# Where attention ends and the MLP begins: the last unit's maxima, four output pieces and one pair of PSUM banks

## The chip, the cores and the metric

The kernel runs on one core of one Trainium2 chip. The metric is the device time of one execution in microseconds (us); the time of a kernel is the median of its timed runs. Beside them one more execution is recorded by the hardware profiler. Its rows have a start, a duration, an engine, a source line of the kernel and the tiles written and read. The engines are PE (TensorE), DVE (VectorE), ACT (ScalarE), POOL (GpSimd) and SP, whose queue starts most DMAs. Each engine works through its own queue in order.

## The reference

One transformer block with adaptive layer norm: attention over the last 512 keys of a cache, then a gated MLP, both added to the residual. Inputs and outputs are float32; D = 576, 2048 queries, 32 query heads on 16 key heads of 128, F = 4608.

```python
mod = (silu(c) @ w_mod).reshape(1, 6, 1, D)           # sa, ca, ga, sb, cb, gb
h = layernorm(x) * (1 + ca) + sa
q = (h @ wq), 32 heads; k, v = last 512 rows of the caches, each head twice
p = softmax(q k^T * 128 ** -0.5)
x = x + ga * ((p v) @ wo)
h = layernorm(x) * (1 + cb) + sb
gate = h @ W_gate; up = h @ W_up
x = x + gb * ((max(gate, 0) * up) @ W_down)
```

## The kernel before

**Precision.** A float32 operand is cut into a rounded part (hi, type fp32r, made by ACT) and the remainder (lo, made by POOL as raw minus hi). A product takes three matmuls: hi by hi, hi by lo, lo by hi.

**Attention.** 128 units, one for each head and each block of 512 queries, u = 0 to 127 (NU = 128). Unit u makes its scores transposed, keys on partitions: two PSUM tiles `s{u}_0` and `s{u}_1` of two banks each, 12 matmuls (lines 462 to 464). DVE reduces them to the maximum of each query (467, 475, 476), PE spreads it over the partitions (490), and `max_bc` (503 to 522) makes of it a tile with the maximum of each query in every partition. `exp_half` (528 to 542) then takes the maxima off and exponentiates, by one of two ways, which `by_pe(u)` chooses:

- PE: the maxima are cut into two parts (512 to 514), transposed (515), rounded by ACT (518), and four matmuls with a matrix of minus ones subtract them inside the PSUM banks (533). ACT's exponential reads the banks (535).
- DVE: one transpose (520), then one DVE subtraction for each half, from PSUM to SBUF (537). ACT's exponential works in SBUF (539).

In this kernel PE does it for u = 0, 1 and for u = 127 (`PE0, PE1 = 2, 1`), DVE for the other 125. After that ACT rounds p to hi (526), DVE and POOL sum over the keys (552, 555), POOL makes lo (546), PE multiplies with V into a `pv` bank (564 to 566) one unit later, DVE divides by the sum (`o_mul`, 572), ACT and POOL cut the result (576 `ohi`, 580 `olo`).

**Output pieces.** `wo_piece(u, q)` multiplies the results of units u - 1 and u (two heads) for 128 queries with two gated blocks of `wo`: 12 matmuls into the pair of banks `psW` (591), then the sum goes to the residual tile `acc`: DVE adds (602), or the bank was filled with `acc` by ACT first (624, a seed) and ACT copies it back (600).

**MLP.** Products of 512 rows and one block of weights, for gate and for up: in each stage m (0 to 35) seven of them, in the order P1, P6, P2, P7, P5, P4, P3, in a Strassen-like scheme in which P2 goes on accumulating in P1's banks and P3 in P5's. A product has two halves (`prod`, line 1046, 7 matmuls each, one for gate and one for up). DVE or ACT then takes it out (`evac`; 1067 or 1069 to 1071 for the gated products P2, P5, P4, P3, of which 1071 is the last; 1175 and 1178 for P6 and P7). ACT and POOL cut the gated result (1061, 1062). Weights of stage m = 1 and after are summed by DVE (852), then cut by ACT (822) and POOL (823, 824). Down products `md_piece` (591, 602) of stage m - 1 stand between the products of stage m.

**The seam.** In stage m = 0 a product's two halves share one tile of two banks, taken from a list:

```python
npair, px, free, kind = [0], {}, ["s", "s"], {}          # 1142
k = free.pop(0)                                          # 1155, in new_banks
free.append(kind[m, s])                                  # 1472, after evac of P6, P2, P7, P4, P3
```

`"s"` means a tile of the pool that held the scores (two tiles, four banks). Stage 0 has no down products, so output pieces that attention left over fill in (`filler`): first three of units 124 and 125, then four of units 126 and 127. The four can only come after the end of unit 127, so the steps are interleaved by hand: P1, P6, then `pv` of unit 127, P2, then `last_unit` (line 1483: spread of the sums, reciprocal 495, transpose 500, `o_mul` 572), `o_hi`, `o_lo`, then `open_x` (1489), which closes the pool of the two banks that held `pv127` and the last spread, `qm128`, opens the pool "x" on these two banks, appends "x" to the list and puts the four pieces into `filler`. P7, P5, P4 and P3 follow. From m = 1 on, `open_g` (1144) replaces the score pool by banks "a" and "b", and "x" and `psW` take the down products in turn.

So P7 took a score pair, P5 the other one and P4 took "x"; the piece of each product stood between its two halves; and P1 of stage 1 (`gh_P`) begins on the pair that P5 and P3 used.

Of the kernel before, what the change touches and what calls it, by code (L numbers as in the profile page):

```python
# [23 lines left out]
EPS = 1e-5  # L24
SCALE = float(P) ** -0.5
H2 = D // 2
PE0, PE1, MLP0 = 2, 1, 8
NLAST = 5


# [1 line left out]
def kernel(  # L32
# [573 lines left out]
    def wo_piece(u1, qt, seed=None):  # L606
        g, qb, h = unit(u1)
        return down_piece([ohi[u1 - 1], ohi[u1]], [olo[u1 - 1], olo[u1]], [wos[h - 1], wos[h]],
                          4 * qb + qt, qt, f"wo{u1}_{qt}", seed=seed)
# [39 lines left out]
    def md_piece(m, k, qt, pool=None):  # L649
        b, fp = divmod(m, NFP)  # L650
        i = 8 * b + 4 * k + qt
        down_piece([hhi[m, f, k] for f in range(2)], [hlo[m, f, k] for f in range(2)],
                   [ds_[m, f] for f in range(2)], i, qt, f"md{m}_{k}_{qt}", pool=pool)()
        if fp == NFP - 1:
            nc.sync.dma_start(out[i * P:(i + 1) * P, :], acc[i])
# [28 lines left out]
    def fast_pieces(m):  # L684
        return ([lambda n=n: fast_piece(m, "4", n) for n in range(2)] +
                [lambda k=k, n=n: fast_piece(m, k, n) for k in ("16", "75", "23") for n in range(4)])
# [83 lines left out]
    def order(m):  # L770
        return ("P1", "P6", "P2", "P7", "P5", "P4", "P3")
# [6 lines left out]
    def flush_stores(left=0, eng=None):  # L778
        while len(stores) > left:
            dst, src = stores.pop(0)  # L780
            (eng or nc.scalar).dma_start(dst.bitcast(F32), src.bitcast(F32))
# [255 lines left out]
    def prod(m, s, n, xx):  # L1037

        hs, w = hop[m // NFP, OPS[s][1]], wop[n]
        ps = pair[m, s][:, xx, :] if m < NG else pair[m, s][xx]  # L1040
        ops = []
        for t in range(2):
            ops += [(w[:, xx, t, :], hs[t]), (w[:, xx, 3 + t, :], hs[t]), (w[:, xx, t, :], hs[3 + t])]
        ops.append((w[0:96, xx, 2, :], hs[2][0:96]))
        for i, (a, c) in enumerate(ops):
            nc.tensor.matmul(ps, a, c, start=s not in ("P2", "P3") and i == 0, stop=i == len(ops) - 1,  # L1046
                             skip_group_check=True)
# [53 lines left out]
    def evac_half(m, s, x):  # L1101
        ps, fast = pair[m, s][x], m in FAST
        if s == "P1":
            if x == 0:
                tmp[m, "q"] = pp.tile([P, 2, 512], F32, tag="hi", name=f"q{m}")
            nc.scalar.copy(tmp[m, "q"][:, x, :], ps)
            if x and m - 1 in FAST:
                fast_last(m - 1)
            return
        q = tmp[m, "q"]  # L1110
        if s == "P6":
            nc.vector.tensor_tensor(q[:, x, :], ps, q[:, x, :], op=ALU.add)
            return
        if s == "P7":
            if x == 0:
                tmp[m, "r"] = pp.tile([P, 2, 512], F32, tag="lo", name=f"r{m}", bufs=2)
            nc.vector.tensor_tensor(tmp[m, "r"][:, x, :], ps, q[:, x, :], op=ALU.add)
            if x:
                nc.scalar.copy(q[:, 1, :], ps)
            return  # L1120
        if s == "P2" and x == 0:
            tmp[m, "r22"] = xp.tile([P, 640], F32, tag="xm", name=f"r{m}")[:, :512]
        if s == "P5" and x == 0:
            tmp[m, "c"] = pp.tile([P, 2, 512], F32, tag="lo", name=f"c22_{m}", bufs=2)
        f, k, r, a, op1 = {"P2": lambda: (0, 0, tmp[m, "r22"], None, ALU.add),
                           "P5": lambda: (1, 1, tmp[m, "c"][:, 0, :], tmp[m, "r"], ALU.add),
                           "P4": lambda: (1, 0, tmp[m, "r"][:, 0, :], tmp[m, "r"], ALU.add),
                           "P3": lambda: (0, 1, q[:, 0, :], q, ALU.subtract)}[s]()
        gated_half(x, ps, r, a, op1)
        if x == 0:  # L1130
            return
        if not fast:
            h_out(m, f, k, r)
        elif s == "P2":
            fast_split(m, "A22", r)
        elif s == "P5":
            fast_split(m, "A11", r)
        elif s == "P4":
            fast_later(m)


    npair, px, free, kind = [0], {}, ["s", "s"], {}
# [6 lines left out]
    def md_pool():  # L1149
        px["n"] = px.get("n", 0) + 1  # L1150
        return (px["x"], "x") if px["n"] % 2 else (psW, "w")
# [6 lines left out]
    def new_pair(m, s):  # L1158
        if m < NG:
            pair[m, s], kind[m, s] = new_banks(f"gu{npair[0]}")  # L1160
            return
        if "g" not in px:
            open_g()
        kind[m, s] = "ab"[(s in ("P6", "P7", "P4")) ^ m % 2]
        pair[m, s] = [px["g"].tile([P, 512], F32, tag=kind[m, s], name=f"gh{m}_{s}_{i}") for i in range(2)]
# [245 lines left out]
    for i in range(4):  # L1411
        m = 2 + 2 * i
# [10 lines left out]
    def sums(m, i):  # L1423

        for k, s in {1: [(0, "S1")], 2: [(0, "S4")], 5: [(1, "S3")], 6: [(1, "S2")]}.get(i, []):
            if 0 < m + k < NFP:
                w_sums(m + k, s)

    def others(m, i):
        w_prep(7 * m + i + 2)  # L1430
        for fn in mextra.pop((m, i - 1, False), []):
            fn()
        for ij in {2: [(1, 0)], 3: [(0, 0)], 4: [(1, 1)], 5: [(0, 1)]}.get(i, []):
            if m + 1 < NFP:
                w_load(m + 1, *ij)

    def mlp_slots():
        for m in range(NB):
            md = [lambda k=k, qt=qt: md_piece(m - 1, k, qt, md_pool())
                  for k in range(2) for qt in range(4)] if m else []  # L1440
            if m - 1 in FAST:
                md = fast_pieces(m - 1)
            for i, s in enumerate(order(m)):
                flush_stores()
                if s not in ("P2", "P3"):
                    new_pair(m, s)
                else:
                    pair[m, s], kind[m, s] = (x[m, {"P2": "P1", "P3": "P5"}[s]] for x in (pair, kind))
                prod(m, s, 7 * m + i, 0)
                if m or i:  # L1450
                    sums(m, i)
                    others(m, i)
                if m >= NG:
                    evac_half(m, s, 0)
                if m and i or m - 1 in FAST:
                    md.pop(0)()
                elif filler and not m:
                    filler.pop(0)()
                for fn in mextra.pop((m, i - 1, True), []):
                    fn()  # L1460
                prod(m, s, 7 * m + i, 1)
                wop.pop(7 * m + i)
                if m >= NG:
                    evac_half(m, s, 1)
                if m and i < 2 or m - 1 in FAST:
                    md.pop(0)()
                elif filler and not i:
                    filler.pop(0)()
                if m < NG:
                    evac(m, s)  # L1470
                if s not in ("P1", "P5") and m < NG:
                    free.append(kind[m, s])
                yield
        for k in range(2):
            for qt in range(4):
                md_piece(NB - 1, k, qt, md_pool())
        flush_stores()
        assert not mextra and not filler

    filler = [lambda q=q: wo_piece(NU - 3, q)() for q in (1, 2, 3)]  # L1480
    mlp = mlp_slots()

    def last_unit():
# [5 lines left out]
    def open_x():  # L1489
        psM_scope.__exit__(None, None, None)  # L1490
        px["x"] = ctx.enter_context(tc.tile_pool(name="psX", bufs=1, space=bass.MemoryType.PSUM,
                                                 reuse_waits="tile"))
        free.append("x")
        filler.extend([lambda q=q: wo_piece(NU - 1, q)() for q in range(4)])


# [49 lines left out]
    step("T.ohi", e + 5, o_hi, NU - 1)  # L1546
    step("T.olo", e + 5, o_lo, NU - 1)
    step("open", e + 6, open_x)

    sched.sort(key=lambda x: x[:2])  # L1550
# [131 lines left out]
```

## Time and profile before

| what | value |
|---|---|
| timed runs | 2923.57, 2925.33, 2927.05 us; median 2925.33 us |
| profiled execution | 2923.07 us, span 2921.3 us |
| mean granted TensorE clock | 0.994 |
| PE busy | 2852.1 us, 98% of the span |
| DVE / ACT / POOL busy | 76% / 49% / 75% |
| HBM | 149 GB/s over the span |
| seam | unit 127's scores begin at 1625.7 us, P1 of stage 1 at 1682.27 us |

The profile's span runs from the first to the last instruction; the execution's own time is 1.8 us longer. A row's bracket tells how long its engine stood idle before it and what released it. PE rows overlap: a matmul of 512 columns lasts 0.39 us, the next starts 0.23 us after it. "Granted clock" is the share of its full clock that TensorE was given in a stretch.

### The profile page before, as it was taken

The page shows a single profiled execution, that of the slowest core. Times are in us where ns is not written, and L with a number is a line of the kernel's source. Part 1 is how long each engine was busy: PE and PEld are TensorE (multiplying, and loading weights), DVE is VectorE, ACT ScalarE, POOL GpSimd, SP SyncE. Part 2 cuts the span into 40 slices and gives each one's busy share as a digit, 9 for nine tenths or more (in the row PEclk, how much of TensorE's full clock was granted, in tenths as well). Part 3 has the DMA queues.
Part 4 walks back from the last instruction along what each step waited for, and adds up shares of the span by engine and source line. Part 5 has one row for each costly group of instructions (what it writes and reads, how often), then busy time and mean ns, then how long its engine had stood idle before and what let it go on. Part 6 is the DMA issues. An engine that isn't in the chain of part 4 may idle for free.

```text
span 2921.3 us, 41631 instructions
## 1 busy us (share of the span) xinstructions
PE 2852.1 (98%) x15206; PEld 2481.5 (85%) x15206; DVE 2211.8 (76%) x3106; ACT 1431.5 (49%) x2023; POOL 2197.3 (75%) x1598
## 2 busy tenths in 40 slices
PE   6899999999999999999999999999999999999999
PEld 4678888888888888888888788888888888888888
DVE  7778888888878888777889677788887566666665
ACT  4666666666676666666656433333333122222221
POOL 5678888888888889876778666677888487777773
PEclk9999999999999999999999999999999999999999
DMA  5222222222223223322143355666767844444443
GB/s 211 87 95 73 83 93 84 67 100 92 92 85 107 88 66 125 109 70 86 66 132 128 118 191 201 218 221 239 263 246 260 319 152 160 153 153 154 154 145 137
DMA packets 165900, 410.62 MB, mean 141 GB/s; under 512 B 15040, under 2 KB 61888, under 8 KB 165696
## 3 DMA queue, kind: packets, MB, share of 16 engines
q1 hardware_dynamic: 132944, 289.23, 30.7%
q10 hardware_dynamic: 32752, 118.73, 10.3%
q8 instruction: 121, 1.98, 0.3%
q14 instruction: 83, 0.68, 0.1%
HBM read 275.81 MB, written 160.40 MB: 149 GB/s over the span
## 4 chain that ended last, share of the span: by engine, by line
PE 83%; POOL 5%; DVE 4%; ACT 3%; DMA 2%; issue 2%; SPq 0%; ACTq 0%; POOLq 0%; DVEq 0%
PE gh_P L1046 23%; PE wo L591 13%; PE qps L388 12%; PE md L591 7%; PE mf L672 6%; PE s L463 3%; PE s L464 3%; PE s L462 3%; PE pv L566 3%; PE pv L565 3%; PE pv L564 3%; POOL lo L546 1%; DMA hx_T<-hb 1%; PE qm L490 1%; DVE t L467 1%
## 5 line engine op out<-in xcount | busy, mean ns | idle before, releaser
L546 POOL TENSOR_TENSOR lo<-p,hi 128x1024 fp32r<-128x1024 f32 x256 | 611.0, 2408 | 2.6 <-ACT hi L526 2.6
L555 POOL TENSOR_TENSOR ks<-ks,p 128x512 f32<-128x512 f32 x256 | 344.1, 1344 | 281.4 <-ACT p L539 210.6
L467 DVE TRANSPOSE_TENSOR_REDUCE t<-s 128x32 f32<-128x1024 f32 x256 | 316.2, 1243 | 133.2 <-PE s L464 122.2
L1046 PE MATMUL gh_P<-hop_B,wop 128*128 128x512 f32 (+1 forms) x1470 | 368.8, 394 | 2.4 <-DVE q L1071 2.4
L1046 PE MATMUL gh_P<-hop_T,wop 128*128 128x512 f32 (+1 forms) x1246 | 315.9, 393 | 0.8 <-DMA wop<-wk_P 0.8
L1046 PEld LDWEIGHTS gh_P<-hop_B,wop 128*128 128x128 f32 (+1 forms) x1470 | 268.4, 189 | 52.7 <-issue 2.8
L537 DVE TENSOR_TENSOR p<-s,mb 128x1024 f32<-128x1024 f32 x250 | 295.3, 1218 | 4.2
L591 PE MATMUL wo<-woga,ohi 128*128 128x288 f32 x1344 | 282.2, 303 | 6.3 <-POOL woga L180 3.8
L388 PE MATMUL qps<-hTa,wA 128*128 128x512 f32 x1176 | 283.9, 393 | 2.3 <-DVE hTa L372 1.7
L526 ACT CAST hi<-p 128x1024 fp32r<-128x1024 f32 x256 | 269.1, 1051 | 7.0
L539 ACT ACTIVATE p<-p 128x1024 f32<-128x1024 f32 x250 | 264.1, 1056 | 16.3 <-DVE p L537 14.4
L388 PEld LDWEIGHTS qps<-hTa,wA 128*128 128x128 f32 x1176 | 222.5, 189 | 49.2 <-ACT lfa L370 2.7
L591 PE MATMUL md<-wogb,hhi 128*128 128x288 f32 x1280 | 260.3, 296 | 0.0
L1046 PEld LDWEIGHTS gh_P<-hop_T,wop 128*128 128x128 f32 (+1 forms) x1246 | 225.3, 188 | 41.1 <-DMA wop<-wk_P 1.2
L442 ACT ACTIVATE qhi<-qps 128x512 fp32r<-128x512 f32 x128 | 76.4, 597 | 340.4 <-PE qps L388 336.9
L591 PEld LDWEIGHTS wo<-woga,ohi 128*128 128x128 f32 x1344 | 219.8, 190 | 14.3 <-POOL woga L180 4.4
L591 PEld LDWEIGHTS md<-wogb,hhi 128*128 128x128 f32 x1280 | 214.0, 188 | 12.1
L591 PE MATMUL wo<-woga,olo 128*128 128x288 f32 x672 | 198.9, 296 | 0.4 <-POOL olo L580 0.2
L602 DVE TENSOR_TENSOR acc<-md,acc 128x576 f32<-128x576 f32 x160 | 120.4, 753 | 101.1 <-PE md L591 100.6
L591 PE MATMUL md<-wogb,hlo 128*128 128x288 f32 x640 | 188.9, 295 | 0.0
L600 ACT COPY acc<-wo 128x576 f32<-128x576 f32 x232 | 147.6, 636 | 68.6 <-PE wo L591 62.2
L580 POOL TENSOR_TENSOR olo<-rb,ohi 128x512 fp32r<-128x512 f32 x128 | 167.0, 1305 | 16.3 <-ACT ohi L576 11.3
(282 smaller groups left out, 7288.7 us busy)
## 6 DMA issues: line engine op xcount, KB each, us to landing
wop<-wk_P SPq DMA_DIRECT2D x133, 640.0 KB
wk_P<-wop ACTq DMA_DIRECT2D x119, 640.0 KB
wr<-wlay SPq DMA_DIRECT2D x68, 384.0 KB
againq<-akq SPq DMA_DIRECT2D x22, 640.0 KB
againo<-ako SPq DMA_DIRECT2D x18, 576.0 KB
rogb<-wd SPq DMA_DIRECT2D x36, 288.0 KB
rwA<-wq SPq DMA_DIRECT2D x32, 320.0 KB
wlay<-wg SPq DMA_DIRECT2D x36, 256.0 KB
```

The lines of the kernel that those rows point to most:

```text
L388: return [lambda i=i, a=a, b=b: nc.tensor.matmul(ps, a, b, start=(i == 0), stop=(i == n - 1)) for i, (a, b) in enumerate(ops)]
L467: nc.vector.tensor_reduce(t4[u][:, 2 * h:2 * h + 2, :].rearrange("p k b -> p (k b)"), t.rearrange("p k (b j) -> p (k b) j", j=32), axis=AX ...
L526: nc.scalar.copy(hi_[u, h], pt[u, h])
L537: nc.vector.tensor_tensor(p, t, bc[u][:, None, :].to_broadcast([P, 2, 512]), op=ALU.subtract)
L539: nc.scalar.activation(p, p, AF.Exp, bias=0.0, scale=1.0)
L546: nc.gpsimd.tensor_sub(lo_[u, h], pt[u, h], hi_[u, h].bitcast(F32))
L555: nc.gpsimd.tensor_tensor(ks_[u], ks_[u], p[:, j, :], op=ALU.add)
L580: nc.gpsimd.tensor_sub(olo[u], o.pop(u), ohi[u].bitcast(F32))
L591: nc.tensor.matmul(ps[:, half, :H2], a[:, sl], w[b][:, cs], start=(n == 0 and seed is None), stop=(n == 5), skip_group_check=seed is not None)
L600: nc.scalar.copy(av, ps[:, :, :H2])
L672: nc.tensor.matmul(ps[:, j, :H2], x[:, sl], w[:, c:c + H2], start=i == 0, stop=i == 2)
L1046: nc.tensor.matmul(ps, a, c, start=s not in ("P2", "P3") and i == 0, stop=i == len(ops) - 1, skip_group_check=True)
```

## The change

Three edits, all at the seam. No DMA, buffer size or matmul of the MLP changes.

1. `PE1` goes from 1 to 0: for u = 127 too, the DVE way of taking the maxima off.
2. The four late output pieces stand behind the second half of P7, P5, P4 and P3, ahead of the product's `evac`, where they stood behind the first half. The three early pieces stay where they were.
3. `open_x` puts "x" at the head of the list. P7 takes "x", P5 and P4 the score pairs; P3 uses P5's.

```diff
-PE0, PE1, MLP0 = 2, 1, 8
+PE0, PE1, MLP0 = 2, 0, 8
...
                 if m and i or m - 1 in FAST:
                     md.pop(0)()
-                elif filler and not m:
+                elif filler and not m and i < 3:
                     filler.pop(0)()
...
                 if m and i < 2 or m - 1 in FAST:
                     md.pop(0)()
-                elif filler and not i:
+                elif filler and not m and (i == 0 or i > 2):
                     filler.pop(0)()
...
-        free.append("x")
+        free.insert(0, "x")
```

## The prediction, made before the run

> **What bounds the kernel now.** I read the page first, then who waited for whom on PE around the seam and behind it, then the timeline row by row, then the granted clock microsecond by microsecond.
>
> ```profile
> PE 2852.1 (98%) x15206; PEld 2481.5 (85%) x15206; DVE 2211.8 (76%) x3106; ACT 1431.5 (49%) x2023; POOL 2197.3 (75%) x1598
> ...
> PE 83%; POOL 5%; DVE 4%; ACT 3%; DMA 2%; issue 2%; SPq 0%; ACTq 0%; POOLq 0%; DVEq 0%
> ```
>
> PE is busy 98% of the span and carries 83% of the chain that ended last. Only what shortens PE's work or its waits counts. PE's waits from 1600 to 1720 us (total, times, longest), the four largest that bear on the change:
>
> ```profile
> PE gh_P L1046 <- DVE q L1071: 2.4, 1, 2.4
> PE wo L591 <- ACT ohi L576: 1.6, 1, 1.6
> PE wo L591 <- ACT acc L600: 1.1, 1, 1.1
> PE wo L591 <- POOL olo L580: 0.8, 1, 0.8
> ```
>
> All those after 1690 us:
>
> ```profile
> PE gh_P L1046 <- POOL wop L824: 1.3, 3, 0.8
> PE mf L672 <- POOL fp_S L699: 0.9, 1, 0.9
> PE gh_P L1046 <- DMA wop<-wk_P: 0.8, 1, 0.8
> ```
>
> The seam holds several waits; the 1200 us behind it hold 3.0 us in all. So a shift of PE at the seam should reach the end almost whole, and the change can be worth a few microseconds, 0.1 to 0.3%. A change under about 0.2% (5.85 us) can't be told from none in a measurement of this kernel.
>
> **Part one: unit 127's maxima by DVE.** Unit 126 does it the DVE way:
>
> ```profile
> 1620.27 0.67 DVE L520 STREAM_TRANSPOSE mb<-r 128x512 f32<-128x512 f32 x1
> 1620.97 2.36 DVE L537 TENSOR_TENSOR p<-s,mb 128x1024 f32<-128x1024 f32 x2
> ```
>
> Unit 127 does it by PE:
>
> ```profile
> 1631.93 1.62 DVE L512 CAST rh<-r 128x16 fp32r<-128x16 f32 x1
> 1634.62 0.62 ACT L518 CAST mr<-mb 128x512 fp32r<-128x512 f32 x1 [6.32 <-DVE mb L515]
> 1634.37 0.40 PE L566 MATMUL pv<-lo,againv 128*128 128x512 f32 x1
> 1636.90 1.02 ACT L535 ACTIVATE p<-s 128x1024 f32<-128x1024 f32 x1
> 1640.91 0.63 ACT L600 COPY acc<-wo 128x576 f32<-128x576 f32 x1
> 1641.60 0.54 PE L591 MATMUL wo<-againo,ohi 128*128 128x288 f32 x2 [1.08 <-ACT acc L600]
> ```
>
> Removed: three small DVE operations (the cast alone 1.62 us), an ACT copy, four matmuls. Added: the two subtractions, 2.36 us. After the change the transpose starts where the cast did, 1631.93; 0.70 later (1620.27 to 1620.97) the first subtraction, which takes half of 2.36, 1.18; the exponential starts at 1633.85 instead of 1636.90. Two things could hold it. ACT: before it stand unit 125's cast, a copy back and a seed, three operations like the 0.63 of L600. They stood behind the ACT copy of the maxima, before which ACT idled 6.32 us; with that copy gone they wait only for the previous output piece, which PE ended before its twelve `pv` matmuls (12 x 0.23, a product's 3.22 / 14, before 1634.6: about 1631.8), so they end by 1633.7. DVE: what is queued behind the subtractions needs the exponential itself. So the gain there is 3.05 us. From the exponential to PE's next wait the chain on ACT stays: two exponentials, two casts, then L600, for which PE waits (1636.90 to 1641.60, 4.7 us). The exponential's form changes by some hundredths; I take **2.95 us** off. PE's piece before that wait runs from 1634.6 to 1636.2, ahead of ACT, so the PE time that the four matmuls free is not gained on top: it becomes wait.
>
> **Part two: P7 on the late banks, pieces behind second halves.** The rows of before, and two pieces of the chain for a product (14 matmuls) and an output piece (12):
>
> ```profile
> 1657.39 1.87 PE L1046 MATMUL gu<-hop_T,wop 128*128 128x512 f32 x7
> 1659.81 0.69 DVE L572 TENSOR_TENSOR rb<-pv,rb 128x512 f32<-128x512 f32 x1
> 1661.30 1.27 POOL L580 TENSOR_TENSOR olo<-rb,ohi 128x512 fp32r<-128x512 f32 x1 [0.40 <-ACT ohi L576]
> 1665.27 0.63 PE L1046 MATMUL gu<-hy_T,wop 128*128 128x512 f32 x2
> ...
> 1668.64 3.22 PE gu L1046 x14
> 1671.86 1.60 PE wo L591 x12
> ```
>
> In before P7's first half starts at 1657.39 without a wait, then the piece waits 1.6 for `ohi` and 0.8 for `olo` (rows above), and P5 starts at 1665.27. With "x" at the head P7 needs the two banks that `o_mul` (L572, ends 1660.50) still reads. The tile is one for both banks, so I let its first matmul wait for both releases. That is a new wait: behind it in PE's queue stand P7, the first late piece and all of the MLP. P7 starts at 1660.50 + 0.14 (the same kind of release takes 0.14 at the stage's end, below) = 1660.64 on the old clock, 3.25 after its old place. P7 and the piece then run 3.22 + 1.60 = 4.82 without a break, since `olo` is there at 1662.57, before the second half ends. P5 starts at 1665.46 instead of 1665.27: **0.2 us worse**. The three waits of before have become one of 3.25 us. The matmuls cost the same wherever they stand, so moving the pieces costs PE nothing; they issue no DMA, and on DVE their addition stood ahead of the product's evacuation already (it only passes the gate multiplication L220).
>
> **Part three: the end of stage 0.** P3 was the last on its pair, and P1 of stage 1 needs just that pair:
>
> ```profile
> 1681.44 0.69 DVE L1071 SCALAR_TENSOR_TENSOR q<-q,gu 128x512 f32<-128x512 f32 x1
> 1682.27 4.82 PE L1046 MATMUL gh_P<-hop_B,wop 128*128 128x512 f32 x14 [2.40 <-DVE q L1071]
> ```
>
> PE waits 2.40 us, and then 14 matmuls take 4.82 instead of 3.22: 1.60 more. The granted clock shows why (stretches of 1 us; the third number from the end is the clock):
>
> ```profile
> 1682.00:1683.00 1.00, 0.73 (x2) 0.66 (x3) 0.12 (x1) 0.84 (x2) 0.15 (x1) 0.50 0.01 5
> 1685.00:1686.00 1.00, 1.00 (x5) 0.86 (x4) 0.00 (x0) 0.41 (x1) 1.00 (x1) 0.88 0.06 26
> ```
>
> Two long waits in attention, each with the clock behind it, show that it isn't certain:
>
> ```profile
> 71.54 0.47 PE L564 MATMUL pv<-hi,kv 128*128 128x512 f32 x1 [2.54 <-DVE ri L495]
> 72.00:73.00 1.00, 1.00 (x7) 0.80 (x6) 0.98 (x1) 0.00 (x0) 1.00 (x2) 1.00 0.00 0
> 183.75 0.71 PE L490 MATMUL qm<-t,quad 128*128 128x80 f32 x2 [2.86 <-DVE t L482]
> 184.00:185.00 1.00, 1.00 (x5) 1.00 (x6) 0.50 (x3) 0.00 (x0) 0.00 (x0) 0.50 0.13 51
> ```
>
> After waits of 2.40 and 2.86 us the clock is halved for some 3 us; after one of 2.54 it is not. Now the change: the pool hands out the pair that was freed first, so P5, and with it P3, should get the pair of P6, and P4 the one of P1 and P2, on which P1 of stage 1 begins. It then needs P4's evacuation, not P3's. P1 follows P4's piece after P3 and its piece, 4.82 us. P4's evacuation now stands behind its piece's addition on DVE:
>
> ```profile
> 1673.49 0.76 DVE L602 TENSOR_TENSOR acc<-wo,acc 128x576 f32<-128x576 f32 x1
> 1675.10 0.69 DVE L1069 TENSOR_TENSOR r<-gu,r 128x512 f32<-128x512 f32 x1 [0.85 <-PE gu L1046]
> 1676.56 0.69 DVE L1071 SCALAR_TENSOR_TENSOR r<-r,gu 128x512 f32<-128x512 f32 x1
> 1677.16 1.51 DVE L852 TENSOR_TENSOR ws<-wr,wr 128x768 f32<-128x768 f32 x1
> 1680.48 1.25 POOL L824 TENSOR_TENSOR wop<-ws,wop 128x512 fp32r<-128x512 f32 x1
> ```
>
> 0.2 to start, 0.76, and 2.15 for its three operations (1675.10 to 1677.25): 3.1 of 4.82, 1.7 spare. P3's evacuation ends as late, 3.1 after the last piece, plus what the weight sum L852 ahead of it delays; P6 of stage 1, which needs that pair, comes after P1 and a down product, 4.82 as well. So **the 2.40 and the 1.60 go**. The weights: P6's are ready 3.06 after their sum (sum ends 1678.67, split 1681.73), sum at 3.1 + 1.51 after P4's piece, together 7.7, needed after 9.64. P7's own evacuation frees "x" long before the first down product.
>
> But part two's wait of 3.25 us is longer than either that halved the clock, so I charge **1.60 us** there.
>
> **Sum.** 2.95 - 0.2 - 1.6 + 2.4 + 1.6 = 5.15 us. The profiled execution, 2923.07 us (span 2921.3 and 1.8 around it), would become 2917.9. It lies 2.26 under the median of the runs, 2925.33; from that the forecast is 2920.2 us, 0.18% faster, and within what can't be told from no change. The least certain term is the clock at P7. The Trainium skill, in "TensorE: Matmul & The Clock Gate", Part 1, states that half rate comes after at least one idle window of some 3.4 us; by that P7's wait would leave the clock alone, the first rival below. The trace disagrees, 0.50 after a wait of 2.40 us, and the measurement decides.
>
> **Rivals.** *No half clock at P7* (0.20). One of the waits quoted, 2.54 us, left the clock at 1.00. Then P7 costs 1.60 less: gain 6.75, 2918.6 us. The sentence of the Trainium skill named above gives this case.
>
> *The banks fall the other way* (0.08). Which pair P5 takes is no row of the trace. On the old pair P1 waits for P3's evacuation, which now starts behind a piece's addition: 0.2 + 0.76 + 2.15 + 0.14 = 3.25 instead of 2.40, with the half clock. 2.95 - 0.2 - 1.6 - 0.85 = 0.3: 2925.0 us.
>
> *The gain is given back downstream* (0.08). PE waits 3.0 us after 1690, on weights cut by POOL and loaded by DMA. If those hold their own pace, each of these waits grows; half of the gain lost gives 2922.8. Against it: what releases them starts from PE's own products, and POOL is 75% busy.
>
> *Slower: DVE falls behind in the last two products of stage 0* (0.04). Weight sums on DVE sometimes take far longer than at the seam (shortest, median, longest in ns):
>
> ```profile
> L852 DVE TENSOR_TENSOR wr<-wr,wr x17: 950/4459/6746, 1672.4 to 2247.4; 128x768 f32<-128x768 f32 x17
> ```
>
> The evacuations now come 2.56 us later (piece 1.60, addition 0.2 + 0.76), and POOL may be at work by then. Two sums of 6.7 us ahead of those of P4 and P3 would add 5.8 and 5.2 to the 0.95 and 1.51 that they took. P1 of stage 1 then waits 5.8 - 1.7 = 4.1 and loses 1.6 to the clock; P3's evacuation ends 3.1 + 5.8 + 6.7 + 0.76 + 2.15 = 18.5 after P4's piece, P6 asks for its pair at 9.64 + 5.7 = 15.3 and waits 3.2. 8.9 lost, net 3.75 slower, 2929.1 us. The sign turns once P4's evacuation comes 5.3 us late (1.7 spare, 1.6 by the clock). Against it: both sums were short at this place.
>
> **How the numbers follow.** My case 0.60, the rivals 0.20, 0.08, 0.08, 0.04. Bounds of my case: part one 2.2 to 3.1 (ACT's three operations late by 0.8, or the form of the exponential costing nothing), half clocks 1.4 to 1.8 each, and timed runs whose wait at the stage's end left the clock alone have 1.6 less to win: 3 to 6.5. The range 2917.3 to 2924.2 holds my case, the clock rival, most of the third; it leaves out the other two and the tails. Over 0.2%: most of the clock rival and a quarter of my case, 0.32. Slower by over 0.2%: 0.03. Within: 0.65.
>
> **What would show it.** No rows of lines 512 to 518 and 533 near 1632 us, two more of L537; the exponential of unit 127 at about 1633.9; PE at L591 about 1638.7 behind L600; one wait of P7 for L572, near 3.2 us, then a clock of 0.50; no wait of line 591 for L576 or L580; `gh_P` of stage 1 near 1677 with no wait on L1071 and clock 1.00. Wrong would be: `gh_P` still waiting for L1071, a wait of PE for L852's weights, or the same seam gain with a later end.

## The result, and the profile after

The change makes the kernel 0.17% faster: median 2919.89 us over 20 runs against 2924.63 us over 20 runs of before, ratio 0.9983, interval 0.9976 to 0.9989. The forecast was 2920.2 us, from 2917.3 to 2924.2, and most likely within 0.2%. Over 20 runs of each kernel the interval stays clear of 1, so a change of 0.17% could be told from none here; the prediction had put that limit at about 0.2%. The profiled execution took 2922.08 us (span 2920.2).

PE's waits of the seam, 1600 to 1720 us, in the changed kernel (total, times, longest):

```profile
PE gu L1046 <- DVE rb L572: 3.0, 1, 3.0
PE qm L490 <- DVE t L482: 0.9, 1, 0.9
PE wo L591 <- ACT acc L600: 0.8, 1, 0.8
```

Two short waits of before, for the seed and for the rounded maxima, are not among the four largest that the prediction shows:

```profile
PE wo L591 <- ACT wo L624: 0.5, 1, 0.5
PE s L533 <- ACT mr L518: 0.5, 1, 0.5
```

Against before, the waits for `ohi`, `olo`, the rounded maxima, the seed and L1071 are gone; one of 3.0 us for L572 is new. The rows of the timeline that belong to it (start, duration, engine, line):

```profile
1631.51 0.45 PE L490 MATMUL qm<-t,quad 128*128 128x80 f32 x2 [0.93 <-DVE t L482]
1633.00 2.35 DVE L537 TENSOR_TENSOR p<-s,mb 128x1024 f32<-128x1024 f32 x2
1634.32 1.06 ACT L539 ACTIVATE p<-p 128x1024 f32<-128x1024 f32 x1 [2.33 <-DVE p L537]
1639.09 0.54 PE L591 MATMUL wo<-againo,ohi 128*128 128x288 f32 x2 [0.76 <-ACT acc L600]
1651.55 3.37 PE L1046 MATMUL gu<-hop_B,wop 128*128 128x512 f32 x14
1657.31 0.69 DVE L572 TENSOR_TENSOR rb<-pv,rb 128x512 f32<-128x512 f32 x1
1658.06 5.06 PE L1046 MATMUL gu<-hop_T,wop 128*128 128x512 f32 x14 [3.01 <-DVE rb L572]
1664.56 0.62 PE L1046 MATMUL gu<-hy_T,wop 128*128 128x512 f32 x2
1676.52 0.69 DVE L1071 SCALAR_TENSOR_TENSOR r<-r,gu 128x512 f32<-128x512 f32 x1
1679.01 3.38 PE L1046 MATMUL gh_P<-hop_B,wop 128*128 128x512 f32 x14
1681.40 0.69 DVE L1071 SCALAR_TENSOR_TENSOR q<-q,gu 128x512 f32<-128x512 f32 x1
1682.22 0.43 PE L591 MATMUL md<-wogb,hhi 128*128 128x288 f32 x2
```

P7's 14 matmuls take 5.06 us behind the wait; P1 of stage 1 takes 3.38 and starts 2.4 us before P3's last evacuation operation begins (1681.40), 1.8 after P4's has ended (1677.21). The granted clock (third number from the end) at P7 and at P1 of stage 1:

```profile
1657.00:1658.00 1.00, 0.00 (x0) 0.00 (x0) 0.96 (x2) 0.07 (x1) 0.85 (x1) 1.00 0.47 193
1659.00:1660.00 1.00, 1.00 (x4) 0.73 (x3) 0.00 (x0) 0.31 (x1) 1.00 (x1) 0.50 0.02 6
1662.00:1663.00 1.00, 1.00 (x6) 0.79 (x5) 0.00 (x0) 0.00 (x0) 0.00 (x0) 1.00 0.56 88
1680.00:1681.00 1.00, 1.00 (x6) 0.83 (x5) 0.90 (x2) 0.10 (x1) 1.00 (x2) 1.00 0.99 400
```

Call the time from unit 127's spread (L490) to the first down product of stage 1 (`md`) the seam: before 1631.14 to 1686.93, 55.79 us; after 1631.51 to 1682.22, 50.71 us. That is 5.08 us less, where 5.15 was reckoned. But this execution's span is only 1.1 us shorter: the start was 0.37 us later, and 3.6 us were lost behind the seam. PE's waits after 1685 us name the place:

```profile
PE gh_P L1046 <- DVE r L1079: 2.3, 1, 2.3
PE gh_P L1046 <- POOL wop L824: 1.5, 2, 1.2
PE mf L672 <- POOL fp_S L699: 0.9, 1, 0.9
PE gh_P L1046 <- DMA wop<-wk_P: 0.7, 1, 0.7
PE gh_P L1046 <- DMA hop_T<-hk_T: 0.5, 1, 0.5
```

and the rows of DVE and POOL around 2175 us the reason:

```profile
2169.47 1.29 POOL L886 TENSOR_TENSOR hx_T<-hx_T 128x512 f32<-128x512 f32 x1 [0.40 <-DMA hx_T<-hb]
...
2171.02 9.55 DVE L852 TENSOR_TENSOR wr<-wr,wr 128x768 f32<-128x768 f32 x1
...
2178.50 1.26 POOL L896 TENSOR_TENSOR hx_T<-hx_T,hy_T 128x512 fp32r<-128x512 f32 x1
2180.50 0.68 DVE L1079 TENSOR_TENSOR r<-gh_P,r 128x512 f32<-128x512 f32 x1
```

A weight sum that takes 0.95 us at its shortest lies on DVE for 9.55 us while POOL works without a gap from 2169.47 to 2179.76, and ends 0.8 us after POOL does. In the first profile of before the sum of this stage took 6.55 us. Whether every execution of the changed kernel loses this is settled by the runs below.

### The profile page after: what moved, and what is told of

It reads as the page before. It is cut to its first block, busy times and chain, and to the rows that moved or that the text cites. A ratio compares the mean times of both kernels' runs of the same rounds, so it can differ in the third digit from the quotient of the medians.

```text
span 2920.2 us, 41623 instructions
## 1 busy us (share of the span) xinstructions
PE 2851.2 (98%) x15202; PEld 2481.4 (85%) x15202; DVE 2226.0 (76%) x3105; ACT 1431.2 (49%) x2022; POOL 2198.7 (75%) x1598
## 4 chain that ended last, share of the span: by engine, by line
PE 87%; DVE 3%; POOL 3%; ACT 2%; DMA 2%; issue 2%; SPq 0%; ACTq 0%; POOLq 0%; DVEq 0%
PE gh_P L1046 25%; PE wo L591 13%; PE qps L388 12%; PE md L591 8%; PE mf L672 6%; PE s L463 4%; PE s L464 4%; PE s L462 3%; PE pv L566 3%; PE pv L565 3%; PE pv L564 3%; POOL lo L546 1%; PE qm L490 1%; ACT p L539 1%; PE gu L1046 1%
## 5 line engine op out<-in xcount | busy, mean ns | idle before, releaser
L600 ACT COPY acc<-wo 128x576 f32<-128x576 f32 x232 | 147.6, 636 | 68.7 <-PE wo L591 62.2
```

What stands on the lines that cost most here:

```text
L600: nc.scalar.copy(av, ps[:, :, :H2])
```

## The experiments

All ratios are against the kernel before on the same chip. They are the recorded ratios, and not always the quotient of two medians: 2916.85 us of "x" second with late pieces, over 2924.08 of before on that chip, is 0.9975, where the recorded ratio is 0.9961. The seam and what is behind it, worked out from two rows and the span of each profile:

| kernel | ratio (interval) | median us | L490 | first `md` | seam | first `md` to the end |
|---|---|---|---|---|---|---|
| before, first profile | | 2924.63 | 1631.14 | 1686.93 | 55.79 | 1234.4 |
| before, again | | one run | 1631.17 | 1687.03 | 55.86 | 1236.6 |
| changed, first profile | 0.9983 (0.9976 to 0.9989) | 2919.89 | 1631.51 | 1682.22 | 50.71 | 1238.0 |
| changed, again | 0.9980 (0.9970 to 0.9990) | 2918.28 | 1632.99 | 1683.71 | 50.72 | 1233.6 |
| edit 1 alone | 0.9984 (0.9975 to 0.9993) | 2920.53 | 1632.80 | 1684.43 | 51.63 | 1238.2 |
| edit 2 alone | 0.9992 (0.9983 to 1.0001) | 2922.80 | 1631.92 | 1687.00 | 55.08 | 1232.8 |
| edit 3 alone | 0.9990 (0.9981 to 0.9999) | 2922.69 | 1631.29 | 1684.84 | 53.55 | 1235.9 |
| edits 1 and 2 | 0.9986 (0.9977 to 0.9995) | 2920.40 | 1632.08 | 1684.28 | 52.20 | 1234.2 |
| changed, PE kept busy | 0.9973 (0.9962 to 0.9984) | 2917.30 | 1631.63 | 1680.77 | 49.14 | 1232.7 |
| changed, "x" second | 0.9974 (0.9964 to 0.9984) | 2916.13 | 1633.42 | 1680.76 | 47.34 | 1233.0 |
| "x" second, late pieces | 0.9961 (0.9948 to 0.9975) | 2916.85 | 1631.74 | 1678.10 | 46.36 | 1237.6 |
| "x" second, a sum on POOL | 0.9990 (0.9981 to 0.9999) | 2921.90 | 1632.42 | 1680.73 | 48.31 | 1244.5 |

Where a kernel was profiled twice its seam repeats to 0.07 us, while what is behind it differs by up to 4.4 us. So the seam is read to a tenth, and the medians, with intervals of about 0.1% to each side, are read for direction: by them alone edit 1 (0.9984) can't be told from the whole change (0.9983).

**Edit 1 alone.**

```diff
-PE0, PE1, MLP0 = 2, 1, 8
+PE0, PE1, MLP0 = 2, 0, 8
```

> Edit 1 alone: unit 127's maxima taken off by VectorE, the pieces and the list as before. My theory (terms add up): PE reaches the second output piece of unit 125 2.95 us earlier and keeps that to the end of stage 0, where the wait of 2.4 us for P3's last evacuation operation and the half clock behind it stay; 2.95 us less, median about 2921.7. The rival, that the first edit only matters together with the others because the shorter chain runs into the next wait (ohi and olo of unit 127), gives under 1 us.

Measured: 0.9984. The seam is 4.2 us shorter, more than 2.95, and the profile says why: the wait at the end of stage 0 is there as before, but this time no half clock followed it. Of the timeline, stage 1's first product (in before 4.82 us behind the same wait):

```profile
1681.09 3.50 PE L1046 MATMUL gh_P<-hop_B,wop 128*128 128x512 f32 x14 [2.40 <-DVE q L1071]
```

Of the windows, the one in which it begins (six matmuls in 1 us, clock 1.00):

```profile
1682.00:1683.00 1.00, 1.00 (x6) 0.81 (x5) 0.00 (x0) 0.33 (x1) 1.00 (x2) 1.00 1.03 400
```

From L490 to this product it is 48.29 us, in before 51.13: 2.84 us by the edit itself, and 1.3 by the clock. The waits for `ohi` and `olo` of unit 127 are 1.6 and 0.8 as before, so the rival falls: the shorter chain carries the whole seam with it.

**Edits 1 and 2, without the list.** The full change with `free.append("x")`.

> Edits 1 and 2 without the list: P7 on a score pair, P4 on x, pieces behind second halves. My theory: P7 starts without a wait; the first late piece waits for olo, some 1.3 us; the wait of P1 of stage 1 for P3's evacuation comes back and is about 3.2 us, behind a piece's addition, with the half clock. Against the full change: 3.0 + 1.8 - 1.3 won, 3.2 + 1.6 lost, about 1.3 us slower, 2921.2. The rival, that the list costs more at P7 than it wins, gives a median below the full change's 2919.9.

Measured: 0.9986, seam 1.49 us longer than the full change's, where 1.3 was expected; `olo` is waited for 0.8 us and not 1.3. The rival falls by the seam; the medians, 2920.40 against 2919.89 and 2918.28 us, would not settle it. Of PE's waits in the seam:

```profile
PE gh_P L1046 <- DVE q L1071: 3.1, 1, 3.1
PE wo L591 <- POOL olo L580: 0.8, 1, 0.8
```

Of the timeline, the product behind the first of them (14 matmuls in 5.04 us, where edit 1 alone has 3.50):

```profile
1679.39 5.04 PE L1046 MATMUL gh_P<-hop_B,wop 128*128 128x512 f32 x14 [3.06 <-DVE q L1071]
```

**Edit 3 alone.** The kernel before with `free.insert(0, "x")`.

> Edit 3 alone: x at the head of the list, maxima by TensorE, pieces behind first halves. My theory: P7 waits 3 us for o_mul, mostly with the half clock behind it (1.8); the piece then waits no more (2.4 us of before gone) and P1 of stage 1 does not wait (2.4 gone, and up to 1.6 of half clock, which the profile of before had and that of the first experiment had not): 0.0 to 2 us less than before, 2923 to 2925. The rival, that the list alone carries the change, gives 2920.

Measured: 0.9990, median 2922.69 us, a little under the 2923 to 2925 expected; seam 2.24 us shorter. My expectation added badly: by the terms on record it is 4.0 at the stage's end minus 1.8 at P7, which is 2.2. The wait at P7 is 3.01 us with the half clock behind it, and L1071 releases nobody.

**Edit 2 alone.** The kernel before with the two conditions on `filler`.

> Edit 2 alone: pieces behind second halves, the rest as before. My theory: the first late piece waits only for olo (0.8 instead of 1.6 and 0.8), P1 of stage 1 waits 3.1 instead of 2.4: 0.9 us less than before at most, 2924.2. The rival, that moving the pieces is what pays since P7's second half covers the wait, gives 2.4 us less and no more wait elsewhere: 2922.6.

Measured: 0.9992, not told apart from no change; seam 0.71 us shorter. `ohi` is no longer waited for, and L1071 is waited for 3.1 us instead of 2.4: the rival, 2.4 us and no more wait elsewhere, falls by the profile. The median, 2922.80 us, is nearer to the rival's 2922.6 than to the 2924.2 expected; before has 2924.08 on this chip, and the intervals are too wide to choose by it. Edits 1 and 3 alone, each by its own terms (2.84 and 2.24), make 5.08 together, as much as all three. So with the list in place the second edit seems to add nothing; that comes from adding up, as no run has edits 1 and 3 without edit 2.

**PE kept busy while P7 waits.** The full change and, ahead of P7, 13 matmuls whose results nobody reads.

```diff
+                if m == 0 and s == "P7":
+                    busy = psW.tile([P, 2, 512], F32, tag="w", name="busy")
+                    for j in range(13):
+                        nc.tensor.matmul(busy[:, j % 2, :], wop[i][:, 0, 0, :], hop[0, "T3"][0],
+                                         start=True, stop=True)
                 prod(m, s, 7 * m + i, 0)
```

> The full change with 13 idle matmuls (operands of P7, into the free psW pair, never read) between P2 and P7, so that PE is busy while P7 waits for its banks. My theory: the halved clock behind the wait comes from the wait itself; with PE busy P7's 14 matmuls take 3.2 us instead of 5.06 at clock 1.00, 1.8 us off the full change: about 2918.0. The rival, that these matmuls are slow for another cause (transfers, SBUF traffic of other engines), leaves 5 us and 2919.9.

Measured: 0.9973, seam 1.57 us shorter than the full change's. PE has 13 matmuls more, and P7 starts 6.51 us after P2, exactly as in the full change (1651.55 to 1658.06 there). Of the timeline:

```profile
1651.66 3.37 PE L1046 MATMUL gu<-hop_B,wop 128*128 128x512 f32 x14
1655.01 3.22 PE L1452 MATMUL busy<-hop_T,wop 128*128 128x512 f32 x13
1658.17 3.50 PE L1046 MATMUL gu<-hop_T,wop 128*128 128x512 f32 x14
```

Of the windows, the one at P7:

```profile
1659.00:1660.00 1.00, 1.00 (x6) 0.83 (x5) 0.00 (x0) 0.43 (x1) 1.00 (x1) 1.00 0.03 12
```

P7 takes 3.50 instead of 5.06 us, with a clock of 1.00 (0.50 in the full change). With PE busy ahead of P7, which begins at the same distance from P2, the half clock is gone: so it comes from PE's standing idle, and this rival falls too.

**"x" second in the list.** The full change with `free.insert(1, "x")`: P7 takes a pair that is long free, P5 and P3 take "x".

> The full change with x put second in the list: P7 takes a score pair, P5 and P3 take x, P4 the pair on which P1 of stage 1 begins. My theory: P7 does not wait (3.0 and the half clock 1.84 gone), the first late piece waits some 1.3 us for olo, P1 of stage 1 does not wait for P3: 3.5 us off the full change, about 2916.4. The rival, that the late x then holds back the first down product (which takes x behind P3's evacuation), gives a new wait there of 1 to 3 us and at most 1 us off. Downstream: if a weight sum on VectorE held behind GpSimd near 2175 us gives part of the gain back, as in the profile of the changed kernel, its row lasts over 8 us and PE waits for L1079; else not.

Measured: 0.9974, seam 3.37 us shorter than the full change's. P7 has no wait, 14 matmuls in 3.48 us; the piece waits only for `olo`:

```profile
1656.84 3.48 PE L1046 MATMUL gu<-hop_T,wop 128*128 128x512 f32 x14
1662.07 0.40 PE L591 MATMUL wo<-againo,olo 128*128 128x288 f32 x1 [0.82 <-POOL olo L580]
1677.55 3.37 PE L1046 MATMUL gh_P<-hop_B,wop 128*128 128x512 f32 x14
```

No wait of a down product for "x" appeared, but there is no room either: the first one starts at 1680.76 us, 0.13 after P3's last evacuation operation has ended (1680.63). Behind the seam nothing was given back here, 1233.0 us.

**"x" second and no piece at P7.** The four late pieces go behind P5's second half, behind P4's, and behind both halves of P3.

```diff
-                elif filler and not m and i < 3:
+                elif filler and not m and i != 3 and (i < 3 or i == 6):
...
-                elif filler and not m and (i == 0 or i > 2):
+                elif filler and not m and (i == 0 or i > 3):
```

> The full change with x second and no piece at P7: the four late pieces behind P5's second half, behind P4's, and behind both halves of P3. My theory: the wait of 0.8 us for olo that the kernel with x second still has goes, and no other comes: 0.8 us less than that kernel, about 2915.3. The rival: P3's two pieces share one pair of banks, and the second waits for the first one's addition behind a weight sum on VectorE, or P3's evacuation comes too late for the first down product: a wait of 1 us or more there and 2916 to 2918.

Measured: 0.9961 over 5 runs, the lowest recorded ratio of all, but not the lowest median: 2916.85 us lies in the rival's 2916 to 2918, not at 2915.3. The rival's wait isn't in the profile, though. The seam is 0.98 us shorter again and has only the waits for L482 and L600 left. In the profiled execution 4.6 us more than in the kernel with "x" second passed behind the seam, with five waits for L824, 2.7 us. Whether it beats that kernel is open: the intervals overlap.

**One weight sum on POOL.** The kernel with "x" second and `S3` of the sums of line 852 on GpSimd.

```diff
-        nc.vector.tensor_tensor(flat(out), flat(a), flat(b), op=op)
+        (nc.gpsimd if s == "S3" else nc.vector).tensor_tensor(flat(out), flat(a), flat(b), op=op)
```

> The kernel with x second, and one of the four weight sums of a stage (the one that lasts longest on VectorE, 4 us in the median and 9.55 us once in the changed kernel's profile) on GpSimd instead. My theory: on VectorE that sum is mostly a wait until GpSimd is idle, so on GpSimd it takes about 2 us, in order; VectorE's rows of it go, no wait of TensorE for L1079 can come, and the stages from 2000 to 2220 us run without it; but GpSimd is 84% busy there and gets 17 x 2 us more, so waits of TensorE for L824 may grow: 2915 to 2920. The rival, that the sums themselves are slow (memory), leaves 4 us a sum on GpSimd and makes it slower by 10 us and more.

Measured: 0.9990, median 2921.90 us, above the 2915 to 2920 expected. The profiled execution is 11.4 us longer behind the seam than the one with the sum on DVE; it took 2926.94 us and is the slowest of the eleven runs, so the typical loss is smaller (the medians differ by 5.8 us, on two chips). In the seam one wait is new: the first down product waits 0.83 us for P3's evacuation. The DVE sum ahead of it lasts 3.25 us here and 1.45 with all sums on DVE. The moved sum's row in the view of line 852 (count; shortest, median, longest in ns), of the kernel with "x" second:

```profile
L852 DVE TENSOR_TENSOR wr<-wr,wr x17: 949/4236/6120, 1670.9 to 2239.8; 128x768 f32<-128x768 f32 x17
```

The same row of this kernel:

```profile
L852 POOL TENSOR_TENSOR wr<-wr,wr x17: 1824/1842/1850, 1671.9 to 2251.1; 128x768 f32<-128x768 f32 x17
```

Of this kernel's waits of PE behind the seam:

```profile
PE gh_P L1046 <- POOL wop L824: 5.7, 5, 2.0
```

On POOL the sum takes 1.84 us every time, on DVE 0.95 to 6.12. So the sum itself isn't slow, and the rival falls as to the cause; that most of its time on DVE is waiting for POOL is read from the rows, such as those around 2175 us above. But 17 x 1.84 = 31 us more on POOL put PE behind the weights (0.4 us of waits for L824 became 5.7).

**Both kernels once more.**

> The changed kernel once more, for a second profile of it. My theory: the seam repeats to a tenth of a microsecond, P7 waits 3.0 us; the wait of 2.3 us for L1079 near 2181 us is a matter of the single execution (a weight sum on VectorE held until GpSimd is idle) and does not repeat at that size; median 2920. The rival, that the earlier seam always brings this wait about, shows it again with a sum of over 8 us near 2171 us.

> The kernel before once more, for a second profile of it. My theory: the wait of 2.4 us at the end of stage 0 repeats; whether the half clock follows depends on the execution (it did in the first profile, not behind the same wait in the first experiment). The rival, that the half clock behind it is fixed by the program, shows 14 matmuls in 4.8 us again.

Measured: the changed kernel's seam is the same to 0.01 us, with the half clock at P7 (5.05 us); its longest sum of that kind is 5.97 us, and no wait for L1079 appears. So the rival falls: the earlier seam doesn't always bring the loss of 3.6 us about. Whether it makes it likelier is open: a wait for L1079 stands in two of the twelve profiles, both with edit 1 (2.3 us in the first of the changed kernel, 1.4 with edit 1 alone), but the time behind the seam doesn't separate the kernels: 1232.7 to 1238.2 us in seven profiles with edit 1 (the one with a sum on POOL left out), 1232.8 to 1236.6 in the four without it. Before has its 2.4 us and the half clock again (14 matmuls in 4.90 us). Of the three profiles with the wait of 2.40 us only that of edit 1 alone was spared.

## Why the prediction was right, point by point

**Part one, 2.95 us.** From L490 to P2 it is 22.90 us in before (1631.14 to 1654.04) and 20.04 after (1631.51 to 1651.55): 2.86. The exponential starts 2.81 us after L490, by the forecast 2.71. ACT's three operations were out of the way in time, and PE reached the piece early and waited for L600, as said: at 1639.09, where 1638.7 was forecast.

**Part two, minus 0.2 and minus 1.6.** From P2 to P5 it is 11.23 us in before (to 1665.27) and 13.01 after (to 1664.56): minus 1.78, against minus 1.8. The wait for both banks was 3.01, where P7 was to start 3.25 later, and the half clock behind it cost 1.57 by the run with PE kept busy, where 1.60 was charged. The prediction says that three waits became one; the rows that it shows for this stretch have two (1.6 and 0.8), and the sum doesn't use the count. The first rival, that the clock stays up, did not hold in any of the three profiles in which P7 waited for L572. Here the sentence of the Trainium skill in "TensorE: Matmul & The Clock Gate", Part 1 (half rate after at least one idle window of some 3.4 us) differs from the measurement: at the seam, waits of 2.4 to 3.1 us were followed by half rate in seven of the eight profiles that have one, and the measurement decides. Other waits, of 2.3 to 2.6 us, did leave the clock at 1.00 (last section).

**Part three, 2.4 and 1.6.** From P5 to the first down product it is 21.66 us in before and 17.66 after: 4.00, as forecast. But the split is not: from P1 of stage 1 to the down product it is 4.66 us in before and 3.21 after, so the half clock there cost 1.45 and not 1.60. The prediction set a row of 4.82, which runs to the end of the last matmul, against 3.22 of the chain, which ends where the next matmul starts. The sum came out the same since the stretch from P5 to P1 is 0.15 us shorter than the wait alone explains; why isn't shown, and that much is luck. The forecast place of `gh_P`, near 1677 us, also contradicts the prediction's own terms: the half clock lies behind its start, so 2.95 - 0.2 - 1.6 + 2.4 = 3.55 ahead of 1682.27 is 1678.7, and it was 1679.01. P1 didn't wait for P3's evacuation, so P5 and P3 had the other pair, and the second rival (the banks fall the other way) fell. In the run without the list it can be seen at its price: a wait of 3.06 where 3.25 was reckoned.

**Passing the gain on.** This was the step with the most luck in it. The median moved by 4.74 us, but the first profile shows one of the prediction's own signs of being wrong, the same gain at the seam with a later end: that execution lost 3.6 of 5.1 again (the third rival). Of these, 2.3 are a wait by the mechanism that the slower rival named, a weight sum on DVE that ends late, only 500 us later than placed there. It was not the rule: the second profile kept all of the gain behind the seam.

**The certainty.** That edit 1 and edit 3 carry everything and edit 2 nothing was in the sum, but not said. The range was given for the median. Single executions spread over 9.55 us, twice the gain (2914.76 to 2924.31 us over the 20 runs), and four of the 20 lie outside the range.

## What to carry to other kernels

Put a new wait where the old one was only if it is shorter: here a pair of banks that came free last was given to the product that ran next, and the same list with that pair one place later saves 3.4 us more of the seam. For a wait of PE of 2.4 to 3 us, reckon not only with its length but with some 1.5 us of half clock behind it (here 1.45 and 1.57), as likely and not as certain, and see whether other work of PE can fill it. When a gain is a tenth of a per cent, read it from the stretch that repeats (the seam, to 0.07 us), and look in a second profile whether a loss elsewhere comes back.

## What was not expected of the hardware

- The half clock behind a short wait isn't fixed by the program: the same wait of 2.40 us at the same place was followed by it in two profiles of before, and not in that of edit 1 alone. The length doesn't decide it either: the wait for L495 near 72 us, 2.49 to 2.56 us, left the clock at 1.00 in all twelve profiles, and so did the 2.33 us for L1079 in the changed kernel's first, while a wait of 1.93 us for a DMA (2307.46 us, edit 1 alone) had 0.63 and 0.50 in the windows of 1 us from 2308 us on. What decides is open. The wait for L1079, and a window behind it:

```profile
2181.32 3.79 PE L1046 MATMUL gh_P<-hop_B,wop 128*128 128x512 f32 x14 [2.33 <-DVE r L1079]
2182.00:2183.00 1.00, 1.00 (x6) 0.62 (x4) 0.96 (x2) 0.00 (x0) 0.00 (x0) 1.00 0.00 0
```

- An addition on DVE with both inputs in SBUF (line 852) lasted 9.55 us where 0.95 is its shortest, through eight POOL operations in a row, and ended 0.8 us after the last of them, when POOL paused.
- Executions differ ahead of the seam (L490 starts at 1631.14 to 1633.42 us, though no edit lies ahead of it) and between the first down product and the stages near 2335 us, but hardly behind these. PE's wait for L699 there is 586.0 to 586.1 us ahead of the end in all twelve profiles; in the first of before:

```profile
2335.27 0.40 PE L672 MATMUL mf<-fw,fp_S 128*128 128x288 f32 x1 [0.94 <-POOL fp_S L699]
```
